# RWKV-6 attention with a GELU MLP on one core: the first tile's y ahead of its state chains, and state chains of fused operations

## The chip, the cores and the metric

One core of a Trainium2 chip runs the whole kernel in one launch. The metric is the device time of that launch in microseconds. A core has a matrix engine (PE; its weight loads are shown as PEld), a vector engine (DVE), a scalar engine (ACT), GpSimd (POOL), and a sync engine (SP) that here only issues DMAs. Matmuls write to PSUM[...]; DVE and ACT read it from there.

## The reference

Attention comes first, then an MLP on its output:

```python
state = np.zeros((B, H, D, D), dtype=np.float32)          # B 4, H 8, S 768, D 48
for t in range(S):
    kt, vt, rt, wt = (k[:, :, t], v[:, :, t], r[:, :, t], w[:, :, t])
    cur = np.einsum('bhd,bhe->bhde', u[None] * kt, vt)
    y[:, :, t] = np.einsum('bhd,bhde->bhe', rt, state + cur)
    state = wt[:, :, :, None] * state + np.einsum('bhd,bhe->bhde', kt, vt)
x = np.ascontiguousarray(y.transpose(0, 2, 1, 3)).reshape(B * S, H * D)
h = x @ w_in                                               # 384 x 2048
g = 0.5 * h * (1.0 + erf(h * inv_sqrt2))
out = g @ w_out                                            # 2048 x 384
```

The inputs are float32 here, and the weights of the MLP come as float64, which the kernel turns into float32 on the chip.

## The kernel before

The tokens are cut into eight tiles of T = 384 (two to a batch entry, so every even tile starts with an empty state). A tile's time is cut further into NC = 6 chunks of C = 64 steps. The eight heads are held as NP = 4 pairs, one head in each half of the 128 partitions. For each tile, `attention` does the following, as a generator that yields between its steps:

- running products of w (`tot`), and the masked products of r and k inside the chunks, which give the matrix `at` (`a_sb`);
- a transpose of k (`kt_ps`, L566), then k times v for each chunk: `kv_ps` (L592);
- the state chain on DVE: the state after chunk c is the one after chunk c - 1 times the chunk's total decay plus that chunk's `kv`. Tile 0 does it with one fused operation (`scalar_tensor_tensor`, L606) per pair and step, after a copy for the first chunk (L617). All other tiles use a multiply over all four pairs (L610) and two additions (L615) per step;
- y inside of chunks (L630): `at` times v, into `y_ps` in PSUM. A tiny DVE copy, `fence` (L634), reads the last columns, so that what comes next waits for these matmuls;
- y across chunks (L648): r times the states, added to the same `y_ps`;
- copies of y into `xT`, the MLP's input. Pairs 0 to 2 are copied directly (L656, L672). Pair 3 goes by ACT to `ysb` (L675) and from there by six small DMAs (L679), three on SP and three on ACT, into the partitions that are left in `xT`.

`mlp` then computes h in 16 blocks (`h_ps`, L726), GELU on ACT (L729), and the output products (`o_ps`, L746 and L860). Its steps are interleaved with the next tile's attention by written lists of step numbers (`place`, `place_next`), so the order on each engine is the program's own order.

Tile 0 has no MLP beside it. It is done in two units of two pairs each, unit 0 (pairs 0 and 1) and unit 1 (pairs 2 and 3), which take turns. From slot 8 on unit 1 goes first. Between the steps `keep_warm` issues matmuls on zeros, which compute nothing (L190). The weights are loaded and turned to float32 in pieces, by `convert` (ACT L291 and L292, DVE L303 to L310). Its last steps are ordered by hand:

```python
for unit, n in ((0, 1), (0, 2), (0, 1), (1, 0), (0, 0), (1, 0), (1, 4)):
    next(units[unit])
    keep_warm(n)
```

Here `units[0]` is unit 1, since the list has been reversed. The order is: chain of unit 1, its inside y, its crossing y and pair 3, chain of unit 0, pair 2's copies, inside y of unit 0, its crossing y and copies. Both units' kv lie ahead of that, in the loop over slots. PSUM is used by tags: `d` has three tiles of two banks (kt, kv, y and the products), `mm` two tiles of one bank (h, o and the warm matmuls).

Of the kernel before, what the change touches and what calls it, by code (L numbers as in the profile page):

```python
# [10 lines left out]
F32 = mybir.dt.float32  # L11
# [6 lines left out]
ALU = mybir.AluOpType  # L18
PSUM = bass.MemoryType.PSUM

C = 64
G = 64
D = 48
T = 384
Q = 2
NC = T // C
N3 = NC // 2
NI = Q * N3
# [3 lines left out]
BANK = 512  # L32
# [12 lines left out]
def kernel(  # L45
# [25 lines left out]
    nc = tc.nc  # L71
# [13 lines left out]
    wk = ctx.enter_context(tc.tile_pool(name="wk", bufs=2))  # L85
    cv = ctx.enter_context(tc.tile_pool(name="cv", bufs=HALFWAY))
    gp = ctx.enter_context(tc.tile_pool(name="gp", bufs=4))
    ps = ctx.enter_context(tc.tile_pool(name="ps", bufs=1, space=PSUM))
    ctx.enter_context(tc.manual_schedule(engines=None))

    half = [slice(0, 64), slice(64, 128)]
    loaded = {}

    def units_of(x):
        return NPART if x == 0 else 1
# [4 lines left out]
    bufs = [io.tile([128, 3 * NP * T], F32, name=f"rkw{i}", bufs=1) for i in range(2)]  # L100
# [83 lines left out]

    nc.scalar.activation(out=zeros[:, 0:1], in_=zeros[:, 0:1], func=AF.Gelu)

    def keep_warm(n):
        t = ps.tile([128, BANK], F32, name="warm", tag="mm", bufs=2) if n else None
        for _ in range(n):
            nc.tensor.matmul(t, lhsT=zeros[:, 0:128], rhs=zeros, start=True, stop=True)  # L190

    keep_warm(8)


# [10 lines left out]
    for h in LEVELS[:-1]:  # L205
# [4 lines left out]
                                op0=ALU.logical_shift_right, op1=ALU.logical_shift_left)  # L210
# [19 lines left out]
    for i, h in enumerate(QUARTERS):  # L230
        for a in range(3):
            w_q = (3 - a) * C // 4
            z = q_ints[1 if a == 0 else 2]
# [45 lines left out]
    def convert():  # L279
        for _ in conversion():  # L280
            pass

    def prepare(upto):
        if not wide:
            return
        for i in range(len(halfway), min(upto, len(raws))):
            words = raws[i].bitcast(U32).rearrange("p (a b) -> p a b", b=2)
            lo, hi = words[:, :, 0], words[:, :, 1]
            f = cv.tile([128, PIECE], U32, name="f")
            e = cv.tile([128, PIECE], U32, name="e")  # L290
            nc.scalar.activation(out=f.bitcast(F32), in_=hi.bitcast(F32), func=AF.Abs)  # L291
            nc.scalar.activation(out=e.bitcast(F32), in_=lo, func=AF.Identity, scale=2.0 ** -51, bias=two)  # L292
            halfway.append((f, e))
# [20 lines left out]
    def attention(x, unit):  # L314

        first = x % HALVES == 0
        parts = range(NPART) if units_of(x) == 1 else range(unit, unit + 1)
        np_ = len(parts)
        qs = np_ * Q
# [6 lines left out]
        at = a_sb[:, :, parts[0] * NI:(parts[0] + np_) * NI]  # L326
# [22 lines left out]
        if x >= 2:  # L349
            for q in range(qs):  # L350
                m_q = slice(q * T // FINE, (q + 1) * T // FINE)
                nc.vector.scalar_tensor_tensor(out=kx[:, 0:n_u].rearrange("p (a m) -> p m a", a=FINE)[:, m_q],
                                               in0=r4[:, m_q], scalar=u_sb[:, q:q + 1], in1=k4[:, m_q],
                                               op0=ALU.mult, op1=ALU.mult)
# [227 lines left out]
        def vs(b, i, g):  # L582
            o = ((parts[b] * NI + i) * 2 + g) * D
            return loaded[x][1][:, o:o + G]

        kvs = []
        for b in range(np_):
            kv_ps = ps.tile([128, 2, BANK], F32, name="kv_ps", tag="d", bufs=3)
            for i in range(NI):
                for p in range(2):  # L590
                    for g in range(2):
                        nc.tensor.matmul(kv_ps[half[g], p, i * D:(i + 1) * D], lhsT=k_t(b, i, p, g),  # L592
                                         rhs=vs(b, i, g)[half[p], 0:D], start=True, stop=True)
# [3 lines left out]
        stq = st[:, 0:NP * NC * D].rearrange("p (q c e) -> p q c e", q=NP, e=D)  # L597
        totq = tot[C].rearrange("p (q c) -> p q c", q=qs)
        stq = stq[:, q0:q0 + qs]
        if not first:  # L600
            b4 = before[:, 0:NP * NC * D].rearrange("p (q c e) -> p q c e", q=NP, e=D)[:, q0:q0 + qs]
        for c in range(NC - 1 + int(first)):
            if x == 0 and c:

                for q in range(qs):
                    nc.vector.scalar_tensor_tensor(out=stq[:, q, c], in0=stq[:, q, c - 1], scalar=totq[:, q, c:c + 1],  # L606
                                                   in1=kvs[0][:, q, c // 2, c % 2], op0=ALU.mult, op1=ALU.add)
                continue
            if c or not first:
                nc.vector.tensor_mul(stq[:, :, c], stq[:, :, c - 1] if c else b4[:, :, NC - 1],  # L610
                                     totq[:, :, c:c + 1].to_broadcast([128, qs, D]))
            for b in range(np_):
                z = stq[:, b * Q:(b + 1) * Q, c]
                if c or not first:
                    nc.vector.tensor_add(z, z, kvs[b][:, :, c // 2, c % 2])  # L615
                else:
                    nc.vector.tensor_copy(out=z, in_=kvs[b][:, :, 0, 0])  # L617
        yield


        def swap(b):
            return parts[b] % 2

        ys = []
        for b in range(np_):
            y_ps = ps.tile([128, 2, BANK], F32, name="y_ps", tag="d", bufs=3)
            for i in range(NI):
                for p in range(2):
                    for g in range(2):
                        nc.tensor.matmul(y_ps[half[g ^ swap(b)], p, i * C:(i + 1) * C], lhsT=vs(b, i, g)[half[p]],  # L630
                                         rhs=at[half[p], g, b * NI + i, :], start=(i == 0), stop=True, skip_group_check=True)

            fence = wk.tile([128, 2], F32, name="fence")
            nc.vector.tensor_copy(out=fence, in_=y_ps[:, :, NI * C - 1])  # L634
            ys.append(y_ps)
        yield

        for i in range(NI):
            for p in range(2):
                for b in range(np_):  # L640
                    q, c3 = divmod(i, N3)
                    for g in range(2):
                        c = 2 * c3 + (p + g) % 2
                        src, c0 = (st, c - 1) if c else (before, NC - 1)
                        if src is None:
                            continue
                        o = ((parts[b] * Q + q) * NC + c0) * D
                        nc.tensor.matmul(ys[b][half[g ^ swap(b)], c % 2, i * C:(i + 1) * C],  # L648
                                         lhsT=src[half[g], o:o + G], rhs=rc[half[g], b, i, c % 2],
                                         start=False, stop=True, skip_group_check=True)  # L650
        if x == 0 and parts[0] == 0:

            for c, copy in enumerate((nc.scalar.copy, nc.vector.tensor_copy)):
                for z in range(2):
                    s = slice(z * G, z * G + D)
                    copy(out=xT[s, 0:Q, :].rearrange("p q (i c t) -> p (q i) c t", c=2, t=C)[:, :, c, :],  # L656
                         in_=ys[0][s, c, 0:NI * C].rearrange("p (i t) -> p i t", t=C))
            yield
            return

        for b in reversed(range(np_)):
            for q in reversed(range(Q)):
                pair = parts[b] * Q + q
                if x == 0 and pair == NP - 2:

                    yield
                y = ys[b][:, :, q * N3 * C:(q + 1) * N3 * C].rearrange("p c (i t) -> p c i t", t=C)
                if pair < NJ:
                    for z in range(2):
                        s = slice(z * G, z * G + D)  # L670
                        copy = nc.vector.tensor_copy if x == 0 else nc.scalar.copy
                        copy(out=xT[s, pair, :].rearrange("p (i c t) -> p c i t", c=2, t=C), in_=y[s])  # L672
                    continue
                ysb = wk.tile([128, T], F32, name="ysb", bufs=1)
                nc.scalar.copy(out=ysb.rearrange("p (i c t) -> p c i t", c=2, t=C), in_=y)  # L675
                for z in range(2):
                    for j in range(NJ):
                        e = z * G + j * (G - D)
                        (nc.scalar if z * NJ + j > (2 if x == 0 else 3) else nc.sync).dma_start(out=xT[z * G + D:(z + 1) * G, j, :], in_=ysb[e:e + G - D, :])  # L679
        yield  # L680

    N_SLOTS = len(LEVELS) + 7
# [187 lines left out]


    units = [attention(0, unit) for unit in range(units_of(0))]
    second = load_second(nc.sync)
    shares = chain(weight_in(gate=True), second, weight_in(gate=True), weight_in(gate=True))
    for unit in units:
        for _ in range(3):
            next(unit)
            keep_warm(3)
            if unit is units[1]:
                next(shares)  # L880
    for slot in range(3, N_SLOTS - 3):
        for _ in range(2):
            next(shares, None)
        if slot == N_SLOTS - 7:
            prepare(1)
        if slot == N_SLOTS - 5:

            units.reverse()
        for unit in units:
            next(unit)  # L890
            keep_warm(2)
    for _ in shares:
        pass
    convert()
    for unit, n in ((0, 1), (0, 2), (0, 1), (1, 0), (0, 0), (1, 0), (1, 4)):
        next(units[unit])
        keep_warm(n)
    convert()
    slots = attention(1, 0)
    next(slots)  # L900

# [92 lines left out]
```

## Time and profile before

| | us |
|---|---|
| median of 6 runs | 610.72 (609.64 to 611.92) |
| the profiled execution | 610.36 |
| its span | 608.5 |
| PE busy | 591.5 (97%) |
| DVE busy | 448.7 (74%) |
| ACT busy | 173.5 (29%) |

All these times are of one core. The span goes from the first instruction to the last; the time of an execution also has what lies around it. A row of the timeline gives start and duration in us, the engine, the line of the kernel, the operation, output and inputs, the shape and how many instructions the row merges; in brackets stands how long the engine was idle ahead of it, and what ended that. A float32 matmul appears as two matmul records and two weight loads. "issue" is idle time in which the engine waited for nothing that the profile shows. What a row gives as the releaser is inferred from semaphores, and can be an instruction that had long ended.

### The profile page before, as it was taken

How to read it: one execution, taken by the hardware profiler on the slowest of the kernel's cores; microseconds unless marked ns; L12 is line 12 of the kernel's file. 1: busy time of each engine (PE TensorE's matmuls, PEld its weight loads, DVE VectorE, ACT ScalarE, POOL GpSimd, SP SyncE). 2: the span in 40 equal slices, each digit the busy share in tenths (PEclk: the TensorE clock that was granted, in tenths of full speed). 3: DMA queues.
4: the chain of work that ended last, by engine and by line, in shares of the span. 5: the costliest groups of instructions: out<-in, count | busy, mean ns of one | idle time of the engine just before them, and what ended most of it. 6: DMA issues, size and time to landing. Idle time of an engine off the chain costs nothing.

```text
span 608.5 us, 15810 instructions
## 1 busy us (share of the span) xinstructions
PE 591.5 (97%) x6916; PEld 445.7 (73%) x6934; DVE 448.7 (74%) x801; ACT 173.5 (29%) x389; POOL 8.4 (1%) x24
## 2 busy tenths in 40 slices
PE   7779999999999999999999999999999999999997
PEld 4556666556699568986699568996699668995694
DVE  8869999998875978588885987679786988520120
ACT  2346476023222322203222232113222232112200
POOL 4100000000000000000000000000000000000000
PEclk9999999999999999999999999999999999999999
DMA  5757348112042305203052304213052002010001
GB/s 203 257 181 234 107 157 300 33 33 77 12 100 79 91 2 109 73 20 92 1 110 73 97 1 80 88 35 91 3 110 72 6 2 40 21 38 0 1 1 40
DMA packets 50565, 46.71 MB, mean 77 GB/s; under 512 B 31680, under 2 KB 35904, under 8 KB 50496
## 3 DMA queue, kind: packets, MB, share of 16 engines
q1 hardware_dynamic: 33152, 29.31, 15.8%
q10 hardware_dynamic: 17344, 16.39, 9.9%
q8 instruction: 55, 0.90, 0.6%
q14 instruction: 14, 0.11, 0.1%
HBM read 36.24 MB, written 4.72 MB: 67 GB/s over the span
## 4 chain that ended last, share of the span: by engine, by line
PE 71%; DMA 1%; issue 0%; DVE 0%; ACTq 0%
PE h_ps L726 31%; PE o_ps L746 29%; PE d L515 4%; PE o_ps L860 2%; PE kv_ps L592 2%; PE y_ps L630 2%; PE y_ps L648 1%; DMA rkw<-kx 1%; PE d L508 1%; DVE o_sb L866 0%; ACTq L462 0%
## 5 line engine op out<-in xcount | busy, mean ns | idle before, releaser
L726 PE MATMUL h_ps<-xT,w_in_sb 128*128 128x384 f32 x768 | 254.1, 489 | 1.4 <-ACT f L291 1.4
L726 PEld LDWEIGHTS h_ps<-xT,w_in_sb 128*128 128x128 f32 x768 | 144.1, 190 | 98.5 <-ACT f L291 1.9
L729 ACT ACTIVATE g<-h_ps 128x384 f32<-128x384 f32 (+1 forms) x128 | 57.2, 449 | 197.8 <-PE h_ps L726 197.8
L746 PE MATMUL o_ps<-t,s 128*128 128x192 f32 x480 | 81.9, 329 | 0.0
L746 PEld LDWEIGHTS o_ps<-t,s 128*128 128x128 f32 x480 | 77.8, 190 | 0.7
L546 DVE COPY_PREDICATED a_sb<-quarter,d 128x384 f32<-128x384 uint8 (+2 forms) x108 | 45.1, 438 | 2.5
L860 PE MATMUL o_ps<-w_out_sb,g 128*128 128x384 f32 x128 | 43.2, 491 | 0.2
L746 PE MATMUL o_ps<-w_out_sb,g 128*128 128x192 f32 x224 | 38.7, 326 | 0.0
L746 PEld LDWEIGHTS o_ps<-w_out_sb,g 128*128 128x128 f32 x224 | 37.0, 190 | 1.9
L860 PEld LDWEIGHTS o_ps<-w_out_sb,g 128*128 128x128 f32 x128 | 23.7, 190 | 17.1 <-DVE w_out_sb L310 1.4
L739 DVE TENSOR_TENSOR s<-g 128x512 f32<-128x512 f32 x14 | 9.4, 670 | 29.1 <-ACT g L729 29.1
L746 PE MATMUL o_ps<-w_out_sb,s 128*128 128x192 f32 x160 | 28.3, 330 | 0.0
L402 PEld LDWEIGHTS d<-rkw 64*64 64x64 f32 x1152 | 18.6, 134 | 12.6 <-DVE rkw L437 7.3
L746 PE MATMUL o_ps<-t,g 128*128 128x192 f32 x160 | 27.6, 326 | 0.0
L339 DVE TRANSPOSE_TENSOR_REDUCE rkw<-kx 128x48 f32<-128x1536 f32 (+3 forms) x24 | 26.8, 1157 | 0.2
L515 PEld LDWEIGHTS d<-kx,rkw 64*64 64x64 f32 x1152 | 24.3, 133 | 3.4 <-DVE a_sb L553 1.6
L515 PE MATMUL d<-kx,rkw 64*64 64x96 f32 x1152 | 26.5, 245 | 0.0
L746 PEld LDWEIGHTS o_ps<-t,g 128*128 128x128 f32 x160 | 26.3, 190 | 0.0
L746 PEld LDWEIGHTS o_ps<-w_out_sb,s 128*128 128x128 f32 x160 | 25.9, 190 | 0.4
L402 PE MATMUL d<-rkw 64*64 64x64 f32 (+1 forms) x1152 | 21.0, 221 | 5.3 <-DVE rkw L437 2.9
L528 DVE TENSOR_TENSOR rkw<-rkw,tot_sb 128x768 f32<-128x768 f32 x12 | 11.5, 959 | 17.3 <-PE d L515 17.3
L375 DVE TENSOR_TENSOR rkw<-rkw 128x384 f32<-128x384 f32 (+2 forms) x24 | 23.6, 1007 | 0.4
(117 smaller groups left out, 641.4 us busy)
## 6 DMA issues: line engine op xcount, KB each, us to landing
rkw<-in_rkw_dram ACTq DMA_DIRECT2D x45, 256.0 KB, 2.8
raw<-in_w_out_dram SPq DMA_DIRECT2D x8, 768.0 KB, 4.4
out_dram<-o_sb SPq DMA_DIRECT2D x21, 192.0 KB, 1.9
raw<-in_w_in_dram SPq DMA_DIRECT2D x5, 768.0 KB, 6.4
v_in<-in_v_dram ACTq DMA_DIRECT2D x5, 584.0 KB, 3.7
raw<-in_w_in_dram SPq DMA_DIRECT2D x9, 256.0 KB, 3.9
rkw<-in_rkw_dram SPq DMA_DIRECT2D x8, 288.0 KB, 3.5
rkw<-in_rkw_dram SPq DMA_DIRECT2D x9, 256.0 KB, 7.4
```

The costliest lines, as they stand in the source:

```text
L339: nc.vector.tensor_reduce(out=fine_sb[:, e, 0:n].rearrange("p a n -> p (a n)"), in_=kx[:, o:o + n * n_m].rearrange("p (m j) -> p m j", j=3 ...
L375: nc.vector.tensor_mul(z, z, by)
L402: nc.tensor.matmul(d[half[p], g, n * width:(n + 1) * width], lhsT=kc[half[g], b, i, p], rhs=right(half[g], b, i, p), start=True, stop=True)
L515: nc.tensor.matmul(d[half[p], g, i * 3 * C // 2:(i + 1) * 3 * C // 2], lhsT=kc[half[g], (n + i) // NI, (n + i) % NI, p], rhs=rx[half[g], 2 ...
L528: nc.vector.tensor_mul(z, z, t2[:, :, 1:2].to_broadcast(z.shape))
L546: nc.vector.copy_predicated(out=an[:, :, :, :, (a + 1) * h:], mask=mask.to_broadcast(data.shape), data=data)
L592: nc.tensor.matmul(kv_ps[half[g], p, i * D:(i + 1) * D], lhsT=k_t(b, i, p, g), rhs=vs(b, i, g)[half[p], 0:D], start=True, stop=True)
L630: nc.tensor.matmul(y_ps[half[g ^ swap(b)], p, i * C:(i + 1) * C], lhsT=vs(b, i, g)[half[p]], rhs=at[half[p], g, b * NI + i, :], start=(i = ...
L726: nc.tensor.matmul(h_ps, lhsT=w_in_sb[:, f // FI, j, f % FI * 128:(f % FI + 1) * 128], rhs=xT[:, j, :], start=(j == 0), stop=(j == NJ - 1))
L729: nc.scalar.activation(out=gs[group][:, f % FG, 0:t], in_=h_ps[:, 0:t], func=AF.Gelu)
L746: nc.tensor.matmul(o, lhsT=lhs(j), rhs=rhs(j), start=start and j == 0, stop=(j == HF - 1), skip_group_check=True)
L860: nc.tensor.matmul(o, lhsT=block(i, f // HF, f % HF), rhs=w_out_sb[:, f, :], start=(f == 0), stop=(f == NF - 1))
```

## The change

In tile 0, y inside of chunks is issued ahead of the state chain of the same unit, and the fence after the chain. Unit 0's y gets two PSUM tiles of one bank each (tag `mm`) in place of one tile of two banks (tag `d`), one for each of the two engines that copy it; it has two fences of one column each. In all other tiles the order stays, and the state chain has one fused operation per pair and step, 20 for five steps, in place of five multiplies and ten additions. The loop over slots ends one slot earlier, so that kv is issued by the order written by hand, after what remains of the loads and the first conversion. The warm matmuls between the last steps (two after each kv, and 1, 2, 1 and 4 in the hand-written order) are replaced by six at the end, in a tile of tag `d`.

```diff
-    def keep_warm(n):
-        t = ps.tile([128, BANK], F32, name="warm", tag="mm", bufs=2) if n else None
+    def keep_warm(n, elsewhere=False):
+        if elsewhere:
+            t = ps.tile([128, 2, BANK], F32, name="warm", tag="d", bufs=3)[:, 0]
+        else:
+            t = ps.tile([128, BANK], F32, name="warm", tag="mm", bufs=2)
...
-        for c in range(NC - 1 + int(first)):
-            if x == 0 and c:
-
-                for q in range(qs):
-                    nc.vector.scalar_tensor_tensor(out=stq[:, q, c], in0=stq[:, q, c - 1], scalar=totq[:, q, c:c + 1],
-                                                   in1=kvs[0][:, q, c // 2, c % 2], op0=ALU.mult, op1=ALU.add)
-                continue
-            if c or not first:
-                nc.vector.tensor_mul(stq[:, :, c], stq[:, :, c - 1] if c else b4[:, :, NC - 1],
-                                     totq[:, :, c:c + 1].to_broadcast([128, qs, D]))
-            for b in range(np_):
-                z = stq[:, b * Q:(b + 1) * Q, c]
+
+        def chain_states():
+            for c in range(NC - 1 + int(first)):
                 if c or not first:
-                    nc.vector.tensor_add(z, z, kvs[b][:, :, c // 2, c % 2])
+                    for q in range(qs):
+                        nc.vector.scalar_tensor_tensor(out=stq[:, q, c], in0=stq[:, q, c - 1] if c else b4[:, q, NC - 1],
+                                                       scalar=totq[:, q, c:c + 1], in1=kvs[q // Q][:, q % Q, c // 2, c % 2],
+                                                       op0=ALU.mult, op1=ALU.add)
                 else:
-                    nc.vector.tensor_copy(out=z, in_=kvs[b][:, :, 0, 0])
-        yield
+                    for b in range(np_):
+                        nc.vector.tensor_copy(out=stq[:, b * Q:(b + 1) * Q, c], in_=kvs[b][:, :, 0, 0])
...
+        split = x == 0 and parts[0] == 0
         ys = []
-        for b in range(np_):
-            y_ps = ps.tile([128, 2, BANK], F32, name="y_ps", tag="d", bufs=3)
-            for i in range(NI):
...
+        def inside():
+
+            for b in range(np_):
+                if split:
+                    y = [ps.tile([128, BANK], F32, name="y_ps", tag="mm", bufs=2) for _ in range(2)]
+                else:
+                    y_ps = ps.tile([128, 2, BANK], F32, name="y_ps", tag="d", bufs=3)
+                    y = [y_ps[:, c] for c in range(2)]
+                for i in range(NI):
...
+                ys.append((y, None if split else y_ps))
+
+        def fences():
+
+            for y, y_ps in ys:
+                fence = wk.tile([128, 2], F32, name="fence")
+                if split:
+                    for c in range(2):
+                        nc.vector.tensor_copy(out=fence[:, c:c + 1], in_=y[c][:, NI * C - 1:NI * C])
+                else:
+                    nc.vector.tensor_copy(out=fence, in_=y_ps[:, :, NI * C - 1])
+
+        if x == 0:
+
+            inside()
+            yield
+            chain_states()
+            yield
+            fences()
+        else:
+            chain_states()
+            yield
+            inside()
+            fences()
+            yield
...
-    for slot in range(3, N_SLOTS - 3):
+    for slot in range(3, N_SLOTS - 4):
...
-    for unit, n in ((0, 1), (0, 2), (0, 1), (1, 0), (0, 0), (1, 0), (1, 4)):
+
+    for unit in (0, 0, 1, 0, 0, 1, 1, 0, 1):
         next(units[unit])
-        keep_warm(n)
+    keep_warm(6, True)
```

## The prediction

> **What bounds the kernel now.** I read the page first, then the busy time by stage, then the timeline of the two stages that the edit touches.
>
> ```profile
> PE 591.5 (97%) x6916; PEld 445.7 (73%) x6934; DVE 448.7 (74%) x801; ACT 173.5 (29%) x389; POOL 8.4 (1%) x24
> ```
>
> ```profile
> 0.00:34.00 34.00, 26.64 (x768) 17.25 (x783) 29.94 (x74) 11.55 (x22) 8.40 (x24) 1.00 0.67 225
> 34.00:46.00 12.00, 8.69 (x239) 6.18 (x238) 7.14 (x29) 4.91 (x7) 0.00 (x0) 1.00 0.60 189
> 46.00:86.00 40.00, 38.72 (x744) 25.26 (x745) 39.23 (x48) 22.49 (x37) 0.00 (x0) 1.00 0.53 165
> 86.00:128.00 42.00, 41.82 (x433) 25.74 (x427) 40.80 (x72) 17.95 (x25) 0.00 (x0) 1.00 0.41 141
> 128.00:560.00 432.00, 430.70 (x4561) 337.71 (x4561) 324.17 (x567) 110.90 (x286) 0.00 (x0) 1.00 0.21 55
> ```
>
> The columns are PE, PEld, DVE, ACT, POOL busy, the granted clock (1.00 throughout), the DMA share and GB/s. From 46 us on PE works without a break, so a microsecond by which the first h_ps matmul starts earlier is a microsecond of the whole. In 34 to 46 nobody is busy: tile 0's state chains and y pass from engine to engine, one step at a time. PE's 8.69 us there even include warm matmuls that compute nothing. This stage is a chain of waits, and the timeline shows it:
>
> ```profile
> 33.16 0.92 PE L592 MATMUL kv_ps<-v_in,kx 64*64 64x48 f32 x48
> 34.50 1.84 DVE L606 SCALAR_TENSOR_TENSOR st<-st,tot_sb,kv_ps 128x48 f32<-128x48 f32 x10
> 34.54 0.92 PE L592 MATMUL kv_ps<-v_in,kx 64*64 64x48 f32 x48
> 36.14 0.67 PE L630 MATMUL y_ps<-a_sb,v_in 64*64 64x64 f32 x26
> 37.56 0.57 PE L630 MATMUL y_ps<-a_sb,v_in 64*64 64x64 f32 x22 [0.75 <-issue]
> 38.18 0.16 DVE L634 COPY fence<-y_ps 128x2 f32<-128x2 f32 x1 [1.84 <-PE y_ps L630]
> 38.54 1.84 DVE L606 SCALAR_TENSOR_TENSOR st<-st,tot_sb,kv_ps 128x48 f32<-128x48 f32 x10
> 38.60 1.38 PE L648 MATMUL y_ps<-rkw,st 64*64 64x64 f32 x40
> 40.03 0.48 ACT L675 COPY ysb<-y_ps 128x384 f32<-128x384 f32 x1 [3.62 <-DVE st L606]
> 40.55 1.12 DVE L672 COPY xT<-y_ps 48x384 f32<-48x384 f32 x2 [0.17 <-ACT ysb L675]
> 41.92 1.38 PE L648 MATMUL y_ps<-rkw,st 64*64 64x64 f32 x40 [0.76 <-DVE fence L634]
> 43.35 0.96 ACT L656 COPY xT<-y_ps 48x384 f32<-48x384 f32 x2 [2.84 <-PE y_ps L648]
> 44.34 1.12 DVE L656 COPY xT<-y_ps 48x384 f32<-48x384 f32 x2 [2.48 <-ACT xT L656]
> 45.68 1.21 PE L726 MATMUL h_ps<-xT,w_in_sb 128*128 128x384 f32 x3 [1.41 <-ACT f L291]
> ```
>
> Three losses are in it. DVE stands idle 1.84 us before its first fence, with the second chain queued behind that fence. PE itself stops for 0.75 us in the middle of a matmul group, waiting for nothing ("issue"). At the end DVE copies the second half of y only after ACT has copied the first. The h_ps wait is put down to ACT's L291, but it starts 0.21 us after the end of DVE's copies (44.34 + 1.12 = 45.46), which release it.
>
> **The change part by part, tile 0.** The built order shows what moves. On PE: kv of unit 1, its inside y, kv of unit 0, crossing 1, inside y 0, crossing 0, six warm matmuls, h_ps. On DVE: chain 1, fence 1, chain 0, pair-2 copies, two fences, copies. ACT, POOL and SP keep their order, with all DMAs (the w_in pieces, the six for xT). The conversion that the loop's end now puts ahead of kv is in the same place on DVE and ACT, since kv issues nothing there. The second DVE copy no longer waits on ACT. Warm matmuls go from 12 to 6; they were issued while PE waited anyway, and the last six (6 x 0.216 us pitch from about 41.4, in the fastest case) end before h_ps is released.
>
> First as if PE never stopped. Kv 1 runs from 33.16 as now; inside y 1 follows from 33.87 (48 records at 0.0148 us pitch), kv 0 ends by 35.6. Chain 1 is unchanged, so fence 1 runs at 36.26 instead of 38.18, and chain 0 right behind it. Crossing 1 takes 1.38 from 36.47, ysb is copied by 38.39, pair 2's copies 38.42 to 39.57, two fences to 39.81, crossing 0 from 39.87, its copies from 41.30 (the 1.435 us from crossing to copy of the trace), both halves at once: 1.12, plus 0.21. h_ps at 42.64 instead of 45.68: **3.04 us**.
>
> Now PE's stop. PE's own code comes in by DMA: the page's q8 moved 0.90 MB in 55 packets, 16 KB each, and PE's 6916 + 6934 records by 55 give 252 instructions a packet. The stop at 36.81 follows a packet that began at 35.26 and took 0.96. An earlier stop of the same kind (0.72 us of "issue" before 26.51) lies some 510 instructions before, two packets' worth, and again PE resumed about 1.4 us after the packet's end. The Trainium skill, "Runtime: NRT & Kernel Launch", section "Instruction fetch mechanics", says the sequencer fetches 256-instruction blocks while it executes the current one, the crossing "mostly hidden". By that rule the sum stays 3.04. The rows speak otherwise while bulk loads fill the DMA engines (share 1.01 in 34 to 36), and I go by them: the code is unchanged up to kv 1, so the next block starts 255 instructions behind kv 1's start and comes at the same time, 37.4 (37.56 before; 36.9 if PE's faster pace asks sooner). Before, that point lay 53 instructions into inside y 1. Now it lies 63 of 96 into kv 0. PE gets there at 35.05 and stands till 37.4. Kv 0 then ends at 37.84, and chain 0 has its data 0.14 later, not behind fence 1. Chain 0 leaves DVE 2.04 later (as 38.26 to 40.29 now): 40.02. Pair-2 copies 1.16: 41.18; fences 0.24; crossing 0 from 41.47; copies 1.435 later, 42.91; 1.12 + 0.21: h_ps at 44.25. Gain **1.4 us**, the value I take; ends 3.04 and, with the block 0.9 later, 0.5. The following block boundary falls 47 instructions into crossing 0, reached at about 42.2; its packet before came at 39.14, so usable by 41.5: a slack of 0.7, small enough to count among the rivals.
>
> DMAs: the third pair into xT landed 3.6 and 3.5 us after issue (45.4, 45.6); the matmul that needs it is h_ps's third, 1.36 after the first. The issues move with ysb, 0.86 earlier, landing at 44.7, needed at 45.6: covered with 0.9 to spare. The next w_in pieces queue behind them on SP as now.
>
> **Tiles 1 to 7.** One step was a multiply and two adds, now four fused operations.
>
> ```profile
> 103.59 0.35 DVE L610 TENSOR_TENSOR st<-st,tot_sb 128x192 f32<-128x192 f32 x1
> 104.05 0.42 DVE L615 TENSOR_TENSOR st<-st,kv_ps 128x96 f32<-128x96 f32 x2
> 107.76 0.55 DVE L303 TENSOR_SCALAR f<-f 128x768 f32<-128x768 f32 x1
> 109.17 8.35 PE L860 MATMUL o_ps<-w_out_sb,g 128*128 128x384 f32 x22
> ```
>
> Five steps took 107.76 - 103.59 = 4.17 us. Ten fused operations took 1.84 with 0.26 for the last, so 0.176 pitch; twenty take 3.52. Each tile saves 0.65 of DVE. From 128 us on DVE has a quarter of its time free and no PE wait there names it for long, so six of the seven tiles give nothing; that cover is the matmul stream. In tile 1 DVE is full: PE's 22 records took 8.35 us, where the 32 from 97.09 took 10.59 (0.326 pitch), so 1.0 us is lost in three waits, two of them on L310. With DVE 0.65 ahead both go: **0.7 us**, between 0 (if something else is as late) and 1.0. Were the fused operations to run without overlap, 0.26 each, a step would take 1.04 instead of 0.83 and tile 1 would lose about 1 us; L606's own starts exclude most of that.
>
> Sum: 1.4 + 0.7 = 2.1 us. The profiled execution has a span of 608.5 in 610.36; it would become 606.4 and 608.3. The median of the runs, 610.72, is 0.36 above the profiled one, so 608.6. What this measurement can tell from no change is 0.2%, 1.2 us.
>
> **Rivals.**
> (a) The code block is there in time, as the rule says: 3.04 + 0.7, 607.0. For it: nothing but the rule; against it, both stops in the rows. Chance 0.15.
> (b) The gain is given back: PE stops again at the boundary in crossing 0 (up to 1 us, directly on the chain), or the block comes late, and tile 1's waits stay. Then 0.3 to 1.0 us remain, 610.1. Chance 0.2.
> (c) Slower, by the clock. "TensorE: Matmul & The Clock Gate", section "HAM oscillation — how this bites in real kernels", warns against PE-idle gaps over about 3.4 us, after which the clock is halved. This speaks against the change: the warm matmuls between the steps go, and PE stands from 35.05 to 37.4, then 1.4 us before crossing 0. In the trace the first warm matmuls, from 2.29 us on, follow each other every 0.42 us until about 5.1, all later ones every 0.216: half rate for some 2.8 us at the start. After that the clock stays 1.00 through gaps up to 1.4. By the rule a gap of 2.4 is still inside its limit and costs nothing; by the rows it is untried. If the clock halves at crossing 0 and returns after one such 2.8 us, 1.4 is lost and the result is level; held for 7 us from 41.5, 3.5 are lost against 2.1 won: 612.1. It decides from about 6.6 us of half clock. Chance 0.1.
> My forecast keeps 0.55.
>
> **How the numbers follow.** Faster by over 0.2%: nearly all of the forecast (0.53) and (a): 0.68. Within: (b) and the forecast's edge: 0.22. Slower: (c): 0.10. The range goes from (a) with tile 1's upper end, 606.6, to (b) with a run's scatter, 611.2, and leaves out (c).
>
> **What would show it.** Right: kv 0's records split about 32 and 16 by an "issue" gap of some 2.3 us near 35 to 37.4; fence 1 at about 36.3; DVE's last copies beside ACT's, not behind; h_ps first at about 44.3; L610's groups of 20 fused operations in 3.6 us; PE's L860 group of 22 near 7.4 us; the clock at 1.00. Wrong: kv 0 whole and h_ps near 42.6 (a); an "issue" gap within crossing 0, or h_ps held by xT's DMAs (b); a clock below 1.00 in 34 to 50 (c).

## The result, and the profile after

| | median, us | ratio to before, same rounds |
|---|---|---|
| before | 610.17 (607.78 to 614.45, 41 runs) | |
| changed | 607.83 (605.17 to 610.00, 20 runs) | 0.9961 [0.9948, 0.9973] |

The changed kernel is faster by 0.39%, 2.4 us; the sum of the prediction was 2.1. The profiled execution took 608.74, with a span of 606.6. Read against the profile of before, however, this one agreement hides several errors, and the point of what follows is to take it apart.

From the page after, the busy times and the granted clock; then the busy time by stage (PE, PEld, DVE, ACT, POOL, clock, DMA share, GB/s):

```profile
PE 591.6 (98%) x6913; PEld 447.0 (74%) x6928; DVE 446.7 (74%) x837; ACT 173.4 (29%) x389; POOL 8.4 (1%) x24
PEclk9989999999999999999999999999999999999999
```

```profile
34.00:44.00 10.00, 7.08 (x267) 6.70 (x268) 6.25 (x28) 2.84 (x4) 0.00 (x0) 0.83 0.59 192
126.00:560.00 434.00, 433.92 (x4572) 339.68 (x4571) 324.19 (x598) 111.42 (x287) 0.00 (x0) 1.00 0.21 54
```

The clock is no longer 1.00 throughout: the third slice has an 8 and 34 to 44 us has 0.83. And from 126 us on PE is busy but for 0.08 of 434 us, where before 1.30 of 432 were missing. The timeline of tile 0, to be laid beside the one of before:

```profile
34.13 0.92 PE L595 MATMUL kv_ps<-v_in,kx 64*64 64x48 f32 x48
34.86 0.89 PE L636 MATMUL y_ps<-a_sb,v_in 64*64 64x64 f32 x48
35.47 1.84 DVE L610 SCALAR_TENSOR_TENSOR st<-st,tot_sb,kv_ps 128x48 f32<-128x48 f32 x10
35.58 0.63 PE L595 MATMUL kv_ps<-v_in,kx 64*64 64x48 f32 x31
37.23 0.15 DVE L648 COPY fence<-y_ps 128x2 f32<-128x2 f32 x1
38.26 0.60 PE L595 MATMUL kv_ps<-v_in,kx 64*64 64x48 f32 x17 [2.05 <-issue]
38.63 2.05 PE L674 MATMUL y_ps<-rkw,st 64*64 64x64 f32 x34
39.20 1.84 DVE L610 SCALAR_TENSOR_TENSOR st<-st,tot_sb,kv_ps 128x48 f32<-128x48 f32 x10
42.99 1.38 PE L674 MATMUL y_ps<-rkw,st 64*64 64x64 f32 x40 [0.86 <-DVE fence L646]
44.41 1.12 DVE L681 COPY xT<-y_ps 48x384 f32<-48x384 f32 x2 [1.47 <-PE y_ps L674]
44.45 0.96 ACT L681 COPY xT<-y_ps 48x384 f32<-48x384 f32 x2 [2.93 <-PE y_ps L674]
45.75 1.21 PE L751 MATMUL h_ps<-xT,w_in_sb 128*128 128x384 f32 x3
```

What was meant is there: inside y 1 directly behind kv 1, the fence 0.03 behind the chain, DVE's last copies beside ACT's. Kv 0 is cut in two, 31 records and 17, by the stop that the prediction placed at 32 and 16. Yet h_ps starts at 45.75, where it was 45.68 before. Two things took the gain away in this execution. Its kv 1 began at 34.13, not 33.16; the start differs between executions of one kernel (33.16 and 35.72 for before, 34.13, 35.16 and 33.36 for the changed kernel in the runs below; here the clock rose at 7.69 us and in the profile of before at 5.11). And crossing 1's first 34 records lasted 2.05 where the 40 took 1.38: the clock is halved there, as the stretches of 3.41 us show that are counted on from its first rise.

```profile
35.00:38.41 3.41, 1.36 (x92) 1.24 (x88) 2.17 (x12) 1.75 (x2) 0.00 (x0) 1.00 0.95 320
38.41:41.82 3.41, 3.41 (x101) 3.41 (x98) 2.37 (x12) 0.48 (x1) 0.00 (x0) 0.50 0.39 148
41.82:45.24 3.42, 2.51 (x58) 1.88 (x54) 1.89 (x6) 0.78 (x2) 0.00 (x0) 1.00 0.37 69
```

So the whole gain of this pair of profiles lies behind h_ps: from there to the end it was 562.80 and is 560.87, 1.93 less. Tile 1 is part of it: before, 22 records took 8.35.

```profile
103.68 3.58 DVE L610 SCALAR_TENSOR_TENSOR st<-st,tot_sb,kv_ps 128x48 f32<-128x48 f32 x20
107.18 0.55 DVE L306 TENSOR_SCALAR f<-f 128x768 f32<-128x768 f32 x1
109.24 7.70 PE L885 MATMUL o_ps<-w_out_sb,g 128*128 128x384 f32 x22
```

Twenty fused operations take 3.58 and DVE's next operation follows at 3.50 instead of 4.17; PE has its records 0.65 sooner. The other 1.28 us was not foreseen: PE waits less for the k blocks that are moved by DMA, at the kv of tiles 2 to 6. One such place, in the timelines of before and after:

```profile
174.40 0.82 PE L592 MATMUL kv_ps<-v_in,rkw 64*64 64x48 f32 x35 [0.77 <-DMA rkw<-kx]
```

```profile
172.73 1.94 PE L595 MATMUL kv_ps<-v_in,rkw 64*64 64x48 f32 x96
```

Taken as what the distance between two starts at that line exceeds its usual value by, and summed over tiles 2 to 6, these waits were 1.72 and are 0.44. Whether the change did that, and what tile 0 is worth when clock and start are the same, had to be found by runs.

### The profile page after: what moved, and what is told of

The parts are those of the page before. It is cut to its first block, busy times and chain, and to the rows that moved or that the text cites. A ratio compares the mean times of both kernels' runs of the same rounds, so it can differ in the third digit from the quotient of the medians.

```text
span 606.6 us, 15833 instructions
## 1 busy us (share of the span) xinstructions
PE 591.6 (98%) x6913; PEld 447.0 (74%) x6928; DVE 446.7 (74%) x837; ACT 173.4 (29%) x389; POOL 8.4 (1%) x24
## 4 chain that ended last, share of the span: by engine, by line
PE 93%; DVE 5%; issue 1%; ACT 0%; DVEq 0%
PE h_ps L751 39%; PE o_ps L771 31%; PE o_ps L885 7%; PE d L518 4%; PE d L405 2%; PE y_ps L674 2%; PE kv_ps L595 2%; PE y_ps L636 2%; DVE rkw L440 2%; PE warm L193 1%; DVE a_sb L450 1%; PE d L511 1%; DVE a_sb L416 1%; PE kt_ps L569 0%; DVE e L309 0%
## 5 line engine op out<-in xcount | busy, mean ns | idle before, releaser
L610 DVE SCALAR_TENSOR_TENSOR st<-st,tot_sb,kv_ps 128x48 f32<-128x48 f32 x160 | 29.0, 258 | 4.2 <-PE kv_ps L595 4.1
L405 PEld LDWEIGHTS d<-rkw 64*64 64x64 f32 x1152 | 18.8, 136 | 12.8 <-DVE rkw L440 7.4
L531 DVE TENSOR_TENSOR rkw<-rkw,tot_sb 128x768 f32<-128x768 f32 x12 | 11.5, 958 | 17.4 <-PE d L518 17.4
```

Of the source, the lines that this page charges most:

```text
L405: nc.tensor.matmul(d[half[p], g, n * width:(n + 1) * width], lhsT=kc[half[g], b, i, p], rhs=right(half[g], b, i, p), start=True, stop=True)
```

## Experiments

**Each part alone.** First only tile 0, with multiply and adds kept in the others; then the kernel before, with the fused chain in every tile.

```diff
-                if c or not first:
+                if x and (c or not first):
+                    nc.vector.tensor_mul(stq[:, :, c], stq[:, :, c - 1] if c else b4[:, :, NC - 1],
+                                         totq[:, :, c:c + 1].to_broadcast([128, qs, D]))
+                    for b in range(np_):
+                        z = stq[:, b * Q:(b + 1) * Q, c]
+                        nc.vector.tensor_add(z, z, kvs[b][:, :, c // 2, c % 2])
+                elif c or not first:
```

> The changed kernel with the multiply and the two additions back in the state chains of tiles 1 to 7; tile 0 stays as changed. Theory A (the sum of the prediction): tile 0 is worth 1.4 us and tile 1's chain 0.7, so this kernel keeps 1.4 us of the gain, about 608.8 where the kernel before has 610.2; its profile again shows the three waits of the output matmuls in tile 1 (22 records in about 8.3 us). Theory B (the profile of the changed kernel shows the first h_ps no earlier than before, 45.75 against 45.68, so that all of the gain lies after it): this kernel has the time before, within 0.5 us.

```diff
-            if x == 0 and c:
-                for q in range(qs):
-                    nc.vector.scalar_tensor_tensor(out=stq[:, q, c], in0=stq[:, q, c - 1], ...
-                continue
             if c or not first:
-                nc.vector.tensor_mul(...)
+                for q in range(qs):
+                    nc.vector.scalar_tensor_tensor(out=stq[:, q, c], in0=stq[:, q, c - 1] if c else b4[:, q, NC - 1],
+                                                   scalar=totq[:, q, c:c + 1], in1=kvs[q // Q][:, q % Q, c // 2, c % 2], ...
```

> The kernel before with the state chains of tiles 1 to 7 as fused operations, and tile 0 untouched. Theory A: 0.7 us faster than before, all of it in tile 1 (22 records of the output matmuls in 7.7 us, not 8.35), and the waits of kv in tiles 2 and 4 for the moved blocks of k (1.0 and 0.7 us in the profile before) stay or go by chance. Theory B: 2 us faster, since the shorter chains also take away the waits of kv in tiles 2 and 4, in every profile.

Measured: tile 0 alone 607.17 (6 runs; 608.8 was expected) against 610.05, 0.9956 [0.9939, 0.9973]; the chain alone 609.37, 0.9991 [0.9978, 1.0004], which cannot be told from no change. Timelines of tile 0 alone and, from tile 1, of it and of the chain alone:

```profile
35.33 0.63 PE L595 MATMUL kv_ps<-v_in,kx 64*64 64x48 f32 x31
38.01 0.45 PE L595 MATMUL kv_ps<-v_in,kx 64*64 64x48 f32 x17 [2.06 <-issue]
44.81 4.11 PE L757 MATMUL h_ps<-xT,w_in_sb 128*128 128x384 f32 x12
...
108.32 8.35 PE L891 MATMUL o_ps<-w_out_sb,g 128*128 128x384 f32 x22
```

```profile
108.24 7.68 PE L853 MATMUL o_ps<-w_out_sb,g 128*128 128x384 f32 x22
```

With the clock at 1.00 it is 6.80 from the end of PE's stop (38.01) to h_ps (44.81), where before it was 8.12 (37.56 to 45.68): 1.32. The group of 22 is 8.35 without the fused chains and 7.68 with them alone: the 0.65 of tile 1 belongs to them. The waits for k blocks do not follow the chains: 0.62 without them here, 0.67 with them alone, against 1.72 and 0.44. That the fused chains remove them is not borne out.

**Where PE stops.** The slot loop's 24 warm matmuls ahead of kv, each cut into thirds or halves (96 or 48 instructions more, the same columns), shift every later instruction against the code blocks of 256.

```diff
         for _ in range(n):
-            nc.tensor.matmul(t, lhsT=zeros[:, 0:128], rhs=zeros, start=True, stop=True)
+            for i in range(pieces):
+                s = slice(i * BANK // pieces, (i + 1) * BANK // pieces)
+                nc.tensor.matmul(t[:, s], lhsT=zeros[:, 0:128], rhs=zeros[:, s], start=True, stop=True)
...
-            keep_warm(2)
+            keep_warm(2, pieces=3 if slot < N_SLOTS - 4 else 1)   # 2 in the other kernel
```

> The changed kernel, with each of the 24 warm matmuls of tile 0's slots 3 to 8 issued as three matmuls on a third of the columns: the same work and nearly the same time, but 96 more PE instructions ahead of kv 1. Theory A (PE's stop is a block of 256 instructions that comes late): the block boundary moves from the middle of kv 0 to 63 instructions into inside y 1, and the one before it is crossed some 4 us earlier, so the block is there: no stop of over 0.5 us between kv 1 and h_ps, kv 1 to the first h_ps takes 9.5 to 10 us instead of 11.6, the clock stays at 1.00, and the time falls by 1.5 to 2 us more than the change itself. Theory C (the stop comes from the order of the work: kv 0's matmuls wait for something there, whatever the count of instructions): the stop stays in kv 0 with about 2 us, and the time is that of the changed kernel.

> As the kernel with 96 more PE instructions, but each warm matmul as two halves: 48 more instructions. Theory A: the stop moves to 15 of 96 instructions into kv 0 (8 of 48 records ahead of it, 40 behind), the block is asked for about 2 us earlier than in the changed kernel, so the stop shrinks from 2.05 us to 0 to 1 us; the time lies between the changed kernel's and the one with 96. Theory C: the stop stays at 32 of kv 0's 48 records, at about 2 us.

Timelines, the 96 first, then the 48:

```profile
43.64 0.58 PE L638 MATMUL y_ps<-a_sb,v_in 64*64 64x64 f32 x25 [2.97 <-issue]
```

```profile
34.79 0.28 PE L597 MATMUL kv_ps<-v_in,kx 64*64 64x48 f32 x7
36.66 0.80 PE L597 MATMUL kv_ps<-v_in,kx 64*64 64x48 f32 x41 [1.59 <-issue]
41.21 0.21 PE L638 MATMUL y_ps<-a_sb,v_in 64*64 64x64 f32 x1 [1.88 <-issue]
43.14 2.74 PE L195 MATMUL warm<-zeros 128*128 128x512 bf16 x6
43.24 1.13 DVE L683 COPY xT<-y_ps 48x384 f32<-48x384 f32 x2 [1.63 <-PE y_ps L676]
```

Counting instructions put the boundaries behind record 8 of kv 0 and 47.5 of y 0 for the 48, and behind 31.5 of y 1 and 23.5 of y 0 for the 96. PE stopped behind record 7 and 47, and behind 31 (a small stop, some 0.3) and 23. In nine traces the stop can be counted outright: it comes behind PE's 861st matmul record (the 860th in the two kernels with warm matmuls left out below), whatever work stands there, and the next one of the two kernels here behind the 989th, which is 128 records or 256 instructions on. (The first traces of before and of the changed kernel, and the two taken side by side, lack some records ahead of it.) So the stop goes where the 256th instruction goes and has nothing to do with kv 0's data or the order of the engines' work. The times that had been expected failed all the same: the boundary behind is then in inside y 0, close to the end of the chain, and PE stops there for 1.9 and 3.0 us. The stop in kv 0 with the 48 was 1.59, where 0 to 1 was expected. Kv 1 to h_ps took 12.3 with the 48 and 13.1 with the 96, where 9.5 to 10 was expected with the 96, and both versions lose what the change won: 609.99, 1.0000 [0.9979, 1.0022], and 612.19, 1.0036 [1.0024, 1.0049]. The clock was halved behind that stop in both, and the six warm matmuls ahead of h_ps then last 2.74 (x6 above) and hold it up: with the 48, DVE's copies end at 44.37 and h_ps starts at 45.67, 1.30 later; in the first profile of the changed kernel, where the clock is back by then, it is 0.22.

**What makes the block late.** The bulk loads (DMA share 0.95 in the stop) were moved away: pieces 2 and 3 of w_in are issued on SP behind the six DMAs into xT.

```diff
-    shares = chain(weight_in(gate=True), second, weight_in(gate=True), weight_in(gate=True))
+    shares = chain(weight_in(gate=True), second, weight_in(gate=True))
...
-    convert()
+    convert(load=False)
...
     keep_warm(6, True)
+    for _ in weight_in():
+        pass
     convert()
```

> The changed kernel with the loads of two weight pieces (0.75 MB each) issued on SP behind the six transfers into xT, in place of ahead of them, so that the DMA engines are quiet from about 35 us to the xT transfers. Theory A (PE's stop is a block of instructions whose packet waits behind the bulk loads): the packet comes within about 1 us, the stop in kv 0 shrinks from 2.05 us to under 0.7, the clock stays at 1.00, and kv 1 to the first h_ps takes 9.5 to 10.3 us instead of 11.6 (10.9 with the clock at 1.00). Some of it may be given back, since ACT then waits for the later piece ahead of the first GELU (up to 1 us). Time 606 to 607.5. Theory D (a block takes its 4 us from the crossing of the block before, whatever the loads do): the stop stays at about 2 us, and the time rises by what ACT waits.

```profile
34.63:38.04 3.41, 1.79 (x123) 1.67 (x116) 2.39 (x13) 1.97 (x3) 0.00 (x0) 1.00 0.11 36
```

```profile
38.21 0.45 PE L596 MATMUL kv_ps<-v_in,kx 64*64 64x48 f32 x17 [1.79 <-issue]
47.55 0.92 ACT L295 ACTIVATE f<-raw 128x768 f32<-128x768 f32 x1 [2.93 <-DMA raw<-in_w_in_dram]
51.96 2.20 PE L752 MATMUL h_ps<-xT,w_in_sb 128*128 128x384 f32 x6 [1.36 <-ACT g L755]
```

By stage and timeline: with a DMA share of 0.11 in this stretch the stop is still 1.79, where the other executions with this boundary have 1.78 to 3.15 at shares of 0.90 to 0.96 during the stop. So theory A does not hold: one of the executions with the loads was as quick, and this is one profile. The loads are not the main cause; what fills the rest of the time is not shown. The version gave back 1.4 us: the late piece kept ACT waiting 2.93, and PE later waited for the GELU behind it (1.36). 608.86, 0.9978 [0.9964, 0.9992].

**The split of the last y.** Unit 0's y in one tile of two banks again.

```diff
-        split = x == 0 and parts[0] == 0
+        split = False
+        last = x == 0 and parts[0] == 0
...
-        if split:
+        if last:
             for c, copy in enumerate((nc.scalar.copy, nc.vector.tensor_copy)):
```

> The changed kernel with unit 0's y in one PSUM tile of two banks again (tag d), so that DVE's copies of it wait for ACT's. Theory A: DVE's copies start 0.98 us later, the first h_ps too, and the time is 1.0 us above the changed kernel's (608.8 against 607.8), still below the kernel before. Rival: the time is the changed kernel's within 0.3 us, because something else (the transfers into xT, the weight piece) ends as late.

```profile
37.52 0.45 PE L595 MATMUL kv_ps<-v_in,kx 64*64 64x48 f32 x17 [2.33 <-issue]
42.88 0.96 ACT L682 COPY xT<-y_ps 48x384 f32<-48x384 f32 x2 [3.22 <-PE y_ps L675]
43.88 1.12 DVE L682 COPY xT<-y_ps 48x384 f32<-48x384 f32 x2 [2.48 <-ACT xT L682]
45.10 1.21 PE L752 MATMUL h_ps<-xT,w_in_sb 128*128 128x384 f32 x3 [0.87 <-ACT f L294]
```

The copies follow one another again, and it is 7.58 from the stop's end to h_ps, with the clock at 1.00: the split is worth 7.58 - 6.80 = 0.78. 608.86, 0.9979 [0.9964, 0.9995].

**Both kernels once more**, for the spread between executions, one execution each.

> The changed kernel once more, for a second profile. Theory A: the stop stands again at record 31 or 32 of kv 0, between 1.5 and 2.5 us long; the three waits of tile 1 are down to one; the waits of kv in tiles 2 and 4 for the moved blocks of k come out otherwise than in the first profile (0.14 and 0.30 us), if they are chance. Whether the clock halves depends on where its window lies: in this run it may not.

> The kernel before once more, for a second profile. Theory A: a stop of PE stands at record 26 of inside y 1, or is absent if the packet came in time; tile 1's three waits are there again (22 records in about 8.3 us); the waits of kv in tiles 2 and 4 (0.98 and 0.74 us) come out otherwise if they are chance. Theory B (the fused chains remove them): they are there again, above 0.6 us each.

```profile
36.61 0.63 PE L595 MATMUL kv_ps<-v_in,kx 64*64 64x48 f32 x31
40.39 0.45 PE L595 MATMUL kv_ps<-v_in,kx 64*64 64x48 f32 x17 [3.15 <-issue]
47.19 4.11 PE L751 MATMUL h_ps<-xT,w_in_sb 128*128 128x384 f32 x12
```

```profile
38.70 0.67 PE L630 MATMUL y_ps<-a_sb,v_in 64*64 64x64 f32 x26
41.77 0.65 PE L630 MATMUL y_ps<-a_sb,v_in 64*64 64x64 f32 x22 [2.39 <-issue]
```

Changed (first fence) 610.2, before 616.13. The places of the stops, 31/17 and 26/22, are those of the first profiles; their lengths are not: 3.15 for 2.05, 2.39 for 0.75. In this execution of before the clock was halved too, from 42.13 to 45.54. The stop's length does not distinguish the two kernels in these profiles, and 616.13 lies above every timed run of before (the highest is 614.96), so this execution of it is no typical one.

The clock does distinguish them, over all timed runs. One halved stretch of 3.41 us takes 0.003 off the mean clock of a run. A mean of 0.997 or less stands in 5 of 160 runs of before, in 11 of 43 of the changed kernel, 7 of 28 with tile 0 alone, 6 of 22 without the split, and in none of 14 with the chain alone. The reordered tile 0 brings it. Whether its order does, or that fewer warm matmuls stand in its last steps, was not separated: no version puts these back.

**Fewer warm matmuls.** The 24 of the slot loop are left out (48 instructions fewer), then also the 18 of the first three steps (84 fewer); none of them feeds a result.

```diff
         for unit in units:
             next(unit)
-            keep_warm(2)
```

> The changed kernel without the 24 warm matmuls of tile 0's slots 3 to 8: 48 PE instructions fewer ahead of kv 1. Theory A (a block of 256 instructions is usable some 4 us after the block before it was entered): the stop leaves kv 0 and stands at record 7 or 8 of the 40 of crossing 1, about 1 us long; chain 0 then starts as soon as fence 1 is done; kv 1 to the first h_ps takes 10.2 to 10.6 us instead of 10.9 to 12.0; the time is 0.4 to 0.8 us below the changed kernel's. Rival: with the warm matmuls gone the clock falls in slots 3 to 8 or in the last steps (a window with PE busy for less than about 1.5 of its 3.4 us), and the time is 1 us or more above the changed kernel's.

> As the kernel without the warm matmuls of slots 3 to 8, and without the 18 of the first three steps of both units as well: 84 instructions fewer than the changed kernel. Theory A: the stop moves on to record 25 of the 40 of crossing 1, about 0.7 us long; kv 1 to h_ps about 10.3 us. Rival: the clock comes later at the start, and kv 1 itself starts 1 us or more later, so that the time is above the kernel without the slots' warm matmuls.

Timeline and stages, without the 24:

```profile
34.83 0.45 PE L674 MATMUL y_ps<-rkw,st 64*64 64x64 f32 x6 [0.99 <-DVE fence L648]
37.52 1.76 PE L674 MATMUL y_ps<-rkw,st 64*64 64x64 f32 x29 [2.25 <-issue]
```

```profile
33.42:36.84 3.42, 0.86 (x36) 0.60 (x27) 3.36 (x20) 1.77 (x2) 0.00 (x0) 1.00 0.99 344
36.84:40.26 3.42, 2.74 (x75) 2.74 (x77) 0.11 (x1) 0.48 (x1) 0.00 (x0) 0.50 0.28 104
```

Boundaries were expected 7 to 8 and 25 records into crossing 1, and came after 6 and 24. The lengths were wrong: stops of 2.25 and 2.56, where 1 and 0.7 were expected, and 12.8 and 15.0 from kv 1 to h_ps, where 10.2 to 10.6 and 10.3 were. The first kernel takes 607.22, 0.9964 [0.9949, 0.9979], much as the changed one does, though its clock was halved in 19 of 22 runs (in this profile for 19.78 to 23.19 as well); the second 609.14, 0.9984 [0.9966, 1.0001], with a halved clock in every run, in the profile for 15.70 to 22.53 and 39.59 to 46.42. Moving the stop, by more instructions or fewer, never removed it.

**The chain behind tile 0, in the same rounds.** The changed kernel beside the one with tile 0 alone.

> The changed kernel, timed on the same chip and in the same rounds as the kernel with only tile 0 changed. Theory A: 0.7 us below that kernel, about 2.1 us below the kernel before. In the profile: the stop at record 31 or 32 of kv 0, 6.8 us from its end to the first h_ps (7.5 with a halved clock), one wait of the output matmuls in tile 1.

> Only tile 0 changed, the multiply and the two additions kept in tiles 1 to 7, beside the changed kernel in the same rounds. Theory A: 1.4 us below the kernel before, 0.7 above the changed kernel. Rival: no difference to the changed kernel (the earlier times, 607.2 against 607.8, would have it so), since what tile 1 saves is less than what the runs scatter by, or is taken back later.

607.46 and 608.10 against 610.51: 0.9955 [0.9936, 0.9973] and 0.9959 [0.9943, 0.9976]. They lie 0.6 apart in the sense expected, but the intervals overlap. The runs without a halved stretch have medians of 606.84 (14 of 22), 607.54 (16 of 22) and, of before, 610.36 (41 of 43); the 0.7 between the first two is not clear of their scatter either. The profile of tile 0 alone has a halved clock this time:

```profile
35.62:39.04 3.42, 1.07 (x75) 0.95 (x68) 2.17 (x12) 1.76 (x2) 0.00 (x0) 1.00 0.94 322
39.04:42.45 3.41, 2.88 (x73) 2.88 (x76) 2.09 (x11) 0.00 (x0) 0.00 (x0) 0.50 0.35 132
```

Together, from the timelines (us; "waits" are those for moved k blocks in tiles 2 to 6, "rest" is h_ps to the end less these):

| kernel, execution | stop | stop's end to h_ps | clock halved behind the stop | h_ps to end | waits | rest |
|---|---|---|---|---|---|---|
| before | 0.75 | 8.12 | no | 562.80 | 1.72 | 561.08 |
| before, again | 2.39 | 9.62 | yes | 562.86 | 1.57 | 561.29 |
| tile 0 alone | 2.06 | 6.80 | no | 561.72 | 0.62 | 561.10 |
| tile 0 alone, side by side | 2.9 | 7.59 | yes | 561.72 | 0.64 | 561.08 |
| changed | 2.05 | 7.49 | yes | 560.87 | 0.44 | 560.43 |
| changed, again | 3.15 | 6.80 | no | 561.14 | 0.89 | 560.25 |
| changed, side by side | 1.8 | 6.81 | no | 560.06 | 0.00 | 560.06 |
| chain alone | none | | no | 560.90 | 0.67 | 560.23 |
| no split | 2.33 | 7.58 | no | 560.66 | 0.24 | 560.42 |

The last column is the clearest answer of the study: four executions without the fused chains have 561.08 to 561.29, five with them 560.06 to 560.43. The kernels with warm matmuls cut or left out have the fused chains too, and 560.07 to 560.83; the one with the loads moved has 561.82, with the 1.36 that PE waits for the late piece in it. The waits scatter across both groups: with cut warm matmuls they were 1.95 and 1.86.

The third column begins at the stop's end and leaves out what comes before. From kv 1's start to h_ps it is 12.5 and 15.7 for before, 11.6, 12.0 and 10.7 for the changed kernel, 10.9 and 12.5 for tile 0 alone, and 11.5 for the chain alone, which has the old order and no stop. A stop of 2 us more or less is worth as much as the new order.

## Why the prediction was right, and where it was not

**Tile 0: right in mechanism, and in size at the full clock.** The step to doubt was PE's stop: it comes at a block boundary, it moved to record 31 where 32 was worked out, and of the 3.04 us without a stop it left 1.3. From the stop's end to h_ps the prediction worked out 6.85 and the runs have 6.80 and 6.81; the gain is 8.12 - 6.80 = 1.32 at the full clock (1.4 forecast), and 9.62 - 7.49 = 2.1 where both are halved (with the untypical execution of before). Of it the split is 0.78; the prediction's own steps had 0.98 for ACT's lead. The rule of the Trainium skill that was set aside, "Runtime: NRT & Kernel Launch", section "Instruction fetch mechanics" (the crossing is "mostly hidden"), fits most of the kernel: from 126 to 560 us of the changed one 36 packets of code came, and PE lost 0.08 us. In tile 0's last steps it fails in 13 of 14 executions; only in the chain alone was y 1 whole and the boundary passed at no cost. Rival (a) falls with it.

**The block's time: right in the first profile, but no constant.** The step had it at 37.4, which is 4.24 behind kv 1's start; it came at 38.26, 40.39 and 37.21, which is 4.13, 5.23 and 3.85 behind it (before: 4.40 and 6.05). The step took for fixed what scatters by 1.4 us or more between executions, of before as well, and kv 1's own start by 2 more. The 0.5 that the prediction kept for a late block is too narrow an end for one execution.

**The clock: wrong.** By "TensorE: Matmul & The Clock Gate", section "HAM oscillation — how this bites in real kernels", a gap of 2.4 was put inside the limit of about 3.4 and costed at nothing; the text called it untried by the rows. A stop of 2.05 sufficed. The gap alone does not decide, since one of 3.15 cost nothing in the second execution of the changed kernel. What goes with it in these runs is PE's busy time within a fixed stretch of 3.41 us: the next stretch was halved after 0.86, 0.92, 0.97, 1.02, 1.07, 1.28, 1.36 and 1.42, and full after every 1.72 and more at the full clock. Between these it does not separate: 1.62, 1.67 and 1.69 were followed by the full clock, and 1.71 by half of it (shown at the end). Tile 0 alone had the 1.62, with the same order of work as the changed kernel's 1.36:

```profile
34.33:37.75 3.42, 1.62 (x111) 1.51 (x104) 2.25 (x13) 1.69 (x3) 0.00 (x0) 1.00 0.93 312
37.75:41.16 3.41, 2.32 (x105) 2.18 (x104) 2.58 (x13) 0.57 (x2) 0.00 (x0) 1.00 0.47 177
```

The price is 7.49 - 6.80 = 0.69, because it returned after one stretch: rival (c) had the right mechanism, but with one stretch of 3.4 us, where it decides from 6.6. Before shows it too (9.62 - 8.12 = 1.5), but in 5 of 160 runs, where the changed kernel does in 11 of 43, so the change paid for part of its gain with it. The text also let the last six warm matmuls end before h_ps is released: at half clock they did not, and h_ps came 1.1 later for it (the versions with 48 and 96 more instructions).

**Tile 1: right.** 0.65 in the trace, forecast 0.7. The group went to 7.70, not to 7.4: three waits became one of 0.17 over the pitch. The 7.4 did not follow from the text's own sum, since 8.35 - 0.7 is 7.65. Twenty fused operations in 3.58, forecast 3.6. Tiles 2 to 7 give nothing of the chain's doing, as said.

**Rival (b), the gain given back:** no stop fell into crossing 0. The DMAs into xT were nearer than said: they landed at 46.51 and 46.72 and were needed at 45.75 + 1.36 = 47.11, so 0.4 to spare and not 0.9.

**The sum.** 1.3 and 0.65 make 2.0, and 2.1 was forecast. But the first pair of profiles comes to its 1.6 (610.36 to 608.74) in another way: the gain in tile 0 was used up by a later start and the clock, and 1.28 came from the k waits, which scatter. The text had PE work without a break from 46 us on; its own rows lack 1.28 of 40 and 1.30 of 432 us, and the k waits lie there. Open is the rest of the medians: tile 0 alone gained 2.4 to 2.9 of the median where its traces show 1.3 or 2.1, the changed kernel at full clock 3.5 in the last rounds (606.84 against 610.36) where the terms make 2.0, and the chain alone 0.6 with an interval that reaches no change, where its trace shows 0.65. That the sum of the medians came out at 2.1 to 2.4 is therefore in part luck: more was gained at full clock than the terms explain, and the clock, put at nothing, took some of it away. With 1 to 3 profiles a kernel and a spread of 2 us in the stop, the traces can't settle that; nor is it known what makes the fetch long, since the loads explain little of it, or what sets the k waits.

No version beats the changed kernel by more than its interval.

## What to carry over

Before costing a reordering in a stage of short dependent steps, count PE's instructions (four for a float32 matmul, two loads and two matmuls; two for the bfloat16 ones that warm the clock) in blocks of 256 and find where the boundary falls in the new order; a stage that gets through 256 in less than the time a block takes to come (3.85 to 6.5 us here) can stop there, as it did in 13 of 14 executions, and in the four versions that shifted the boundary the stop moved and did not go. Ask of the same stage how long PE is busy per 3.41 us when warm matmuls go, and read the clock of all runs, not only of the profiled one. And split a difference between two profiles at a point behind the stage (here h_ps), repeat both kernels, and believe a term only if it separates the groups, as 561.1 and 560.3 do, however well the sum agrees.

## What was not expected of the hardware

The time from entering a block to PE's going on in the next was 3.85 to 6.5 us in the executions with a stop, in spite of a packet that itself takes 0.9 to 1.2: it began 1.2 (loads moved away) to 4.1 us (96 more instructions) after the crossing, and PE resumed about 1.4 after its end. In the chain alone the packet began at 33.08, ahead of kv 1's start at 33.29, and PE did not stop; what sets the packet's start is not shown.

The clock was halved in whole stretches of 3.41 us, eight times after a stretch with PE busy for 1.42 or less and once after 1.71, in the kernel without the 24 warm matmuls:

```profile
16.36:19.78 3.42, 1.71 (x100) 1.43 (x95) 3.42 (x8) 0.00 (x0) 1.64 (x3) 1.00 0.63 199
19.78:23.19 3.41, 3.12 (x116) 2.94 (x114) 3.41 (x10) 1.82 (x2) 0.00 (x0) 0.50 0.73 225
```

No gap between two groups of matmuls was over 1.4 us there. The clock was back after one halved stretch in seven of nine cases. In the kernel without 42 warm matmuls both halvings lasted two stretches; PE was busy for 2.80 and 2.40 of the first, while a halved stretch with 2.73 was enough in another kernel. So PE's busy time comes near to what decides here, and is not shown to be it.
